# The last output tile in three pieces on two store queues, and three input loads issued as two DMAs each

## The chip, the cores and the metric

The kernel runs on one core of a Trainium2 chip. Its time is the device time of an execution in microseconds (us). TensorE (PE in the profile) does the matrix products; VectorE (DVE), ScalarE (ACT) and GpSimd (POOL) do elementwise work; SyncE (SP) computes nothing here and issues DMAs. ScalarE and GpSimd can issue DMAs too.

## The reference

Two layers in a row: a decayed linear attention, and a two-layer perceptron on its output. Inputs and output are float32.

```python
B, H, S, D = 4, 8, 768, 64                # attention, in blocks of 64 positions
for b in range(S // 64):
    intra = einsum('bhic,bhjc->bhij', qb, kb) * Dmask      # lam ** (i - j), i >= j
    intra = einsum('bhij,bhjd->bhid', intra, vb)
    inter = einsum('bhid,bhde->bhie', qb * lam_pow, kv_state)
    out[:, :, block] = intra + inter
    kv_state = lam_block * kv_state + einsum('bhsd,bhse->bhde', kb * rev_pow, vb)
x = out.transpose(0, 2, 1, 3).reshape(3072, 512)
h = x @ w_in                               # 512 -> 2048
g = h + sin(alpha * h) ** 2 / (alpha + 1e-9)
result = g @ w_out                         # 2048 -> 512, output (3072, 512)
```

## The kernel before, in words

**Tiles and stages.** The 3072 rows of the perceptron are worked in six groups g of 512. The attention comes in 24 units u, four to a group, each one half of the heads for 256 positions of one batch. For a unit, q, k and v come in as three loads of 256 KB (`ld{u}q`, `ld{u}k`, `ld{u}v`, issued by `load`, line 467, on SP's queue, each into one of three staging slots of its kind), are cast to bfloat16 (`cq`, `ck`) or scaled (`sv`), and q and k are transposed, in later units by a DMA transpose (`dt{u}`, line 519). The matmuls of a unit are `step{u}` on TensorE; `oe` writes its part of the transposed activations `xt`.

For each group, sixteen `f1_g_f` (four matmuls of 128x512 each, line 684) make one 128-row slice of the hidden layer in PSUM; `sn` takes the sine (line 694), `sq` the square (line 699), and `g` puts the sum into slice f of the tile `gall` (line 707). Then four output tiles m of 128 rows follow: `f2_g_m_j`, j = 0 to 3, adds four of the sixteen slices each (`f2mm`, line 712), `ev` copies the result from PSUM to an output tile `ob` in SBUF (line 729), and `out_g_m` stores it (`f2st`, line 748) in two DMAs of 64 rows, one for each parity of the row.

**Order.** The order on every engine is written out by hand: the table `SEQ` lists the operations of PE, DVE, ACT, POOL and SP. `Plan.run` (line 47) walks these five lists with estimated durations; it chooses buffers and PSUM banks (`take`, `give`) and the order in which the program is emitted, not the order on an engine. Four PSUM banks `f` and three `part` tokens limit the running sums, three slots the output tiles. The framework puts in the semaphores from what reads and writes what.

**The end.** The last output tile to be computed is (g, m) = (5, 3). `make_f2_end` (line 935) makes it in two halves of 256 columns: `f2_5_3_0a` to `3a` early, in the middle of other tiles, evicted by ACT as `end0`, stored by `send0`; and `f2_5_3_0b` to `3b` as the very last matmuls, evicted by DVE as `end1` into an output tile of its own, stored by `send1`, whose two DMAs go to SP's queue and ACT's. Just before them on TensorE stands the tile (5, 0): `ev_5_0` on ACT, `out_5_0` in two DMAs on SP.

The end of the program (line 1067 in the profile) waits on SP for the semaphores of all DMAs.

Of the kernel before, what the change touches and what calls it, by code (L numbers as in the profile page):

```python
# [12 lines left out]
FP32 = mybir.dt.float32  # L13
# [16 lines left out]
class Plan:  # L30
# [11 lines left out]
    def add(self, *a, **k):  # L42
        op = Op(*a, **k)
        self.ops.append(op)
        return op
# [100 lines left out]
def kernel(  # L146
# [12 lines left out]
    P = nc.NUM_PARTITIONS  # L159
# [4 lines left out]
    NG = B * S // 512  # L164
    HH = H // 2
    HP = H // 2
    DM, DFF = moe_w_in.shape
# [38 lines left out]
        "DVE":  # L206
# [17 lines left out]
        "ACT":  # L224
# [52 lines left out]
    }  # L277
    QS = set()
    CK0 = [("ACT", .62), ("DVE", .43)]
    RING = 3  # L280
    NQK = 4
    NQT = 4
# [35 lines left out]
    outp = ctx.enter_context(tc.tile_pool(name="outp", bufs=1))  # L318
# [4 lines left out]
    V, G, A, SY = nc.vector, nc.gpsimd, nc.scalar, nc.sync  # L323
# [3 lines left out]
    def where(u):  # L327
        g, r = divmod(u, 4)
        bb, hh = divmod(r, 2)
        tp, bp = divmod(g, 2)  # L330
        return g, tp, 2 * bp + bb, bb, hh

    plan = Plan({"f": ["f0", "f1", "f2", "f3"], "s": ["s"], "okv": ["okv"],
                 "st0": list(range(RING)), "st1": list(range(RING)), "st2": list(range(RING)),
                 "qk": list(range(NQK)), "qt": list(range(NQT)),
                 "vb": list(range(NVB)), "sm": list(range(NSM)), "s1": list(range(NML)),
                 "s2": list(range(NML)), "ob": list(range(NOB)), "part": list(range(NPART))})
    add = plan.add
# [9 lines left out]
    def slot(op, pool_, kind, shape, dt, name=None):  # L348
        name = name or kind
        return pool_.tile(shape, dt, name=name, tag=f"{name}{op.bank[kind][0]}")  # L350

    def sync_dep(ins, after):
        tc.add_manual_dep(ins.ins, after.ins.name, mybir.DependencyInfo(
            mybir.DependencyClass.Sync, mybir.DependencyReason.DATA))
# [28 lines left out]
    for c in range(2):  # L383
# [4 lines left out]
        out=mask[:], in0=it[:].rearrange("p two e -> p (two e)").unsqueeze(1)  # L388
# [66 lines left out]
    def load_w_in(op, a, w):  # L455
        op.ins = G.dma_start(
            out=w_in_sb[:, :, a:a + w],
            in_=moe_w_in[:, a:a + w].rearrange("(c p) g -> p c g", p=P))

    def load_w_out(op, a, n):  # L460
        op.ins = G.dma_start(
            out=w_out_sb[:, a:a + n, :],
            in_=moe_w_out[a * P:(a + n) * P, :].rearrange("(f p) d -> p f d", p=P))
# [3 lines left out]
    def load(op, u, i, gate):  # L467
        _, tp, b, _, hh = where(u)
        src = (q, k, v)[i]
        tl = slot(op, stagep, f"st{i}", [P, HH, 2, D], FP32, "st_" + "qkv"[i])  # L470
        src = src[b, hh * HH:(hh + 1) * HH, tp * W:(tp + 1) * W, :]
        op.ins = SY.dma_start(
            out=tl[:].rearrange("p h two e -> p (h two e)"),
            in_=src.rearrange("h (p two) e -> p h (two e)", two=2))
        if gate is not None:
            sync_dep(op.ins, gate.ins)
        T[u, "qkv"[i]] = tl

    def cast(op, u, j):
        if j == 0:  # L480
            T[u, "qk"] = slot(op, work, "qk", [P, 2, 2, HH, D], BF16)
        o = T[u, "qk"][:, j]
        i = T[u, "qk"[j]][:].rearrange("p h two e -> p two h e")
        if j == 0 and u in QS:
            hh = where(u)[4]
            ENGINE[op.eng].tensor_tensor(
                out=o, in0=i, in1=E[:, :, hh * HH:(hh + 1) * HH].unsqueeze(3)
                .to_broadcast([P, 2, HH, D]), op=ALU.mult)
        elif op.eng == "ACT":
            A.copy(out=o, in_=i)  # L490
        else:
            ENGINE[op.eng].tensor_copy(out=o, in_=i)  # L492
# [219 lines left out]
    def f2mm(op, first, g, m, j, cols=slice(0, DM)):  # L712
        if j == 0 and op.lent is None:
            op.tile = bank(op, "f", [P, DM], FP32, "ops")
        elif j == 0:
            kind, i, head = op.lent
            if kind == "s":
                op.tile = ps.tile([P, DM], FP32, name="ops", tag=f"s{i}")
            else:
                if i == 0:  # L720
                    head.both = new_okv(head)
                op.tile = head.both[:, i]
        n = NFC // 4
        for f in range(j * n, (j + 1) * n):
            op.ins = nc.tensor.matmul(  # L725
                out=first.tile[:, cols], lhsT=gall[g][:, f, m * P:(m + 1) * P],
                rhs=w_out_sb[:, f, cols], start=(f == 0), stop=(f == NFC - 1))
# [2 lines left out]
        op.tile = slot(op, outp, "ob", [P, DM], FP32)  # L730
        A.copy(out=op.tile[:], in_=first.tile[:])  # L731

    def f2end(op, first, cols):
        op.tile = slot(op, outp, "ob", [P, DM], FP32)
        o = op.tile[:, cols]
        if op.eng == "ACT":
            A.copy(out=o, in_=first.tile[:, cols])
        else:
            V.tensor_copy(out=o, in_=first.tile[:, cols])

    def f2send(op, ev, g, m, cols, queues):
        _, tp, b, _, _ = where(4 * g + 2 * (m // 2))
        r0 = b * S + tp * W + (m % 2) * C
        rows = out[r0:r0 + C, cols].rearrange("(p two) d -> two p d", two=2)
        for par in range(2):
            queues[par].dma_start(out=rows[par], in_=ev.tile[par * D:(par + 1) * D, cols])

    def f2st(op, ev, g, m):
        _, tp, b, _, _ = where(4 * g + 2 * (m // 2))
        r0 = b * S + tp * W + (m % 2) * C  # L750
        rows = out[r0:r0 + C, :].rearrange("(p two) d -> two p d", two=2)
        for par in range(2):
            SY.dma_start(out=rows[par], in_=ev.tile[par * D:(par + 1) * D, :])


    PEL = 0.22
    on = lambda e, c: [(e, c)]
    for i in range(NWARM):
# [8 lines left out]
        first = dop if i <= NLAM else first  # L767
# [36 lines left out]
    def make_unit(u):  # L804
        _, tp, b, bb, hh = where(u)
        lq, lk, lv = ld[u]
        early = u < NT
        cq = add(f"cq{u}", CQS if u in QS else CQ if u else CK0, [lq, tbm if u in QS else None],
                 lambda op: cast(op, u, 0), take=("qk",), give=((lq, "st0"),),
                 gives={"qk": 3 if u not in DMAT else 2})  # L810
        ck = add(f"ck{u}", CK if u else CK0, [lk, cq], lambda op: cast(op, u, 1),
                 give=((lk, "st1"),))
# [121 lines left out]

    def make_f2_end(g, m):
        prev = None
        for k, cols in enumerate((slice(0, DM // 2), slice(DM // 2, DM))):
            first = None
            for j in range(4):
                deps = [f1_done[g, f][None] for f in range(4 * j, 4 * j + 4)]  # L940
                op = add(f"f2_{g}_{m}_{j}{'ab'[k]}", on("PE", .44), deps + [prev], None,
                         take=("f", "part") if j == 0 else (), lag=PEL if j == 3 else -0.05, mode="n")
                first = first or op
                op.emit = lambda op, j=j, first=first, cols=cols: f2mm(op, first, g, m, j, cols)
                prev = op
            if k == 0:
                ev = add("end0", on("ACT", .4), [prev], lambda op, first=first, cols=cols:
                         f2end(op, first, cols), take=("ob",), give=((first, "f"), (first, "part")))
                add("send0", on("SP", 1.0), [ev], lambda op, ev=ev, cols=cols:
                    f2send(op, ev, g, m, cols, (SY, SY)))  # L950
            else:
                ev = add("end1", on("DVE", .35), [prev], lambda op, first=first, cols=cols:
                         f2end(op, first, cols), take=("ob",))
                add("send1", on("SP", 1.0), [ev], lambda op, ev=ev, cols=cols:
                    f2send(op, ev, g, m, cols, (SY, A)))

    def make_f2(g, m):
# [39 lines left out]
    for x in WX:  # L997
        j, a = done[x], at[x]
        n = (WI if x == "i" else WO)[j]
        if x == "i":  # L1000
            op = add(f"wi{j}", on("POOL", .8), [],
                     lambda op, a=a, n=n: load_w_in(op, a, n), dma=(NDC * P / 16 * dw(n), dw(n)))
            wi.update((f, op) for f in range(a // P, (a + n) // P))
        else:
            op = add(f"wo{j}", on("POOL", .2 * n), [],
                     lambda op, a=a, n=n: load_w_out(op, a, n), dma=(n * P / 16 * .081, .081))
# [65 lines left out]
```

## Time and profile before

| What | Value |
|---|---|
| Time, median of three runs | 215.83 us (215.66 to 216.15) |
| Span of the profiled execution, first to last instruction | 214.5 us |
| Median less that span | 1.3 us |
| TensorE, busy share of the span | 96% |
| ScalarE, VectorE, GpSimd | 65%, 56%, 61% |
| Granted TensorE clock | 1.000 |
| HBM read, written | 27.27 MB, 6.29 MB |

The profile comes from one execution; its own time is given as the span. What lies outside the span, before the first and after the last instruction, is in the timed runs alone. Times in a view count from the span's start. An instruction line of the timeline reads: start, length, engine, source line, operation, tiles. "SPq" and "ACTq" are DMAs being issued; the data move later.

### The profile page before, as it was taken

Reading aid. Unit: us, or ns where it says so; the run is one execution under the profiler, and the core shown is the slowest. Engines: PE = TensorE matmul, PEld = TensorE weight load, DVE = VectorE, ACT = ScalarE, POOL = GpSimd, SP = SyncE. Lnnn points to the kernel's source line nnn. Section 1 sums busy time; section 2 is a strip of 40 time slices with the busy share of each in tenths; the row PEclk is TensorE's granted clock in tenths of the full one; section 3 lists DMA queues with packets and bytes.
Section 4 is the critical chain, followed back from the end, with each engine's and each line's share of the span. In section 5 each row is a group of like instructions: output and inputs, shape, how many; then the busy total and the mean of one; then the engine's idle time right before and its main releaser. Section 6 shows DMA issues by size and latency. Waiting matters only on the chain.

```text
span 214.5 us, 5205 instructions
## 1 busy us (share of the span) xinstructions
PE 205.4 (96%) x2037; PEld 106.5 (50%) x2066; DVE 119.4 (56%) x174; ACT 138.8 (65%) x251; POOL 131.2 (61%) x212
## 2 busy tenths in 40 slices
PE   8988999999999999999999999999999999999992
PEld 3666444455445555455555555554444444444551
DVE  2387775466488774676968868766455313212100
ACT  3574788555799668878888789466578746335030
POOL 7899899288899699898979998430441030003000
PEclk9999999999999999999999999999999999999999
DMA  5999999999999999999966743040240022041553
GB/s 156 300 288 202 209 180 158 290 237 292 280 262 246 218 195 191 326 283 234 263 169 161 176 92 68 3 89 16 44 98 2 0 52 49 0 93 43 112 121 78
DMA packets 62139, 33.65 MB, mean 157 GB/s; under 512 B 17938, under 2 KB 59170, under 8 KB 62114
## 3 DMA queue, kind: packets, MB, share of 16 engines
q1 hardware_dynamic: 57776, 29.04, 57.8%
q0 software_dynamic: 4224, 4.19, 12.5%
q8 instruction: 16, 0.26, 0.5%
q10 hardware_dynamic: 114, 0.07, 0.1%
q14 instruction: 9, 0.07, 0.1%
HBM read 27.27 MB, written 6.29 MB: 156 GB/s over the span
## 4 chain that ended last, share of the span: by engine, by line
PE 91%; DVE 2%; ACT 2%; POOL 2%; issue 1%; DVEq 0%
PE hps L689 37%; PE ops L725 35%; PE sp L532 3%; PE okv L725 3%; PE okv L655 3%; PE bz L762 3%; PE okv L642 2%; PE pt L508 1%; DVE gall L708 1%; PE okv L566 1%; POOL vb L498 1%; ACT s L696 1%; ACT s L703 1%; DVE sm L540 1%; PE kp L566 0%
## 5 line engine op out<-in xcount | busy, mean ns | idle before, releaser
L708 DVE SCALAR_TENSOR_TENSOR gall<-s,r_sb,hps 128x512 bf16<-128x512 bf16 (+1 forms) x97 | 69.6, 739 | 59.7 <-ACT s L703 42.5
L689 PE MATMUL hps<-xt,w_in_sb 128*128 128x512 bf16 (+1 forms) x367 | 90.2, 377 | 1.8 <-DVE gall L708 0.5
L696 ACT ACTIVATE s<-hps,alpha_sb 128x512 bf16<-128x512 f32 (+1 forms) x97 | 65.5, 680 | 28.2 <-PE hps L689 27.2
L725 PE MATMUL ops<-w_out_sb,gall 128*128 128x512 bf16 (+1 forms) x362 | 82.1, 370 | 0.6 <-issue 0.5
L705 POOL TENSOR_TENSOR s<-s 128x512 bf16<-128x512 bf16 x31 | 32.2, 1042 | 48.0 <-ACT s L696 45.7
L725 PEld LDWEIGHTS <-gall 128*128 128x128 bf16 x400 | 38.5, 98 | 42.1 <-DVE gall L708 0.2
L689 PEld LDWEIGHTS <-w_in_sb 128*128 128x128 bf16 x388 | 36.4, 98 | 42.0 <-issue 1.7
L703 ACT ACTIVATE s<-s 128x512 bf16<-128x512 bf16 (+1 forms) x66 | 40.3, 621 | 1.2
L540 DVE TENSOR_TENSOR sm<-sp,mask 128x1024 bf16<-128x1024 f32 x24 | 29.2, 1217 | 1.2 <-PE sp L532 1.2
L498 POOL TENSOR_TENSOR vb<-st_v,R 128x512 bf16<-128x512 f32 x24 | 25.0, 1046 | 2.0 <-DMA st_v<-in_v_dram 2.0
L731 ACT COPY ob<-ops 128x512 f32<-128x512 f32 x21 | 12.2, 585 | 19.2 <-PE ops L725 16.2
L594 POOL TENSOR_TENSOR kvbd<-kvx,LBD 128x256 bf16<-128x256 f32 x32 | 19.6, 614 | 2.5
L674 DVE TENSOR_TENSOR xt<-okv,ET 128x512 bf16<-128x512 f32 x24 | 16.5, 686 | 6.3 <-ACT kva L576 4.0
L591 POOL TENSOR_TENSOR kvx<-kva,kvs 128x128 f32<-128x128 f32 x32 | 14.6, 457 | 7.1 <-ACT kva L576 7.0
L492 POOL CAST qk<-st_k 128x512 bf16<-128x512 f32 x18 | 10.9, 615 | 4.1 <-DMA st_k<-in_k_dram 4.0
L532 PE MATMUL sp<-qt 64*64 64x128 bf16 x384 | 10.2, 221 | 0.5 <-DVE sm L540 0.3
L490 ACT CAST qk<-st_q 128x512 bf16<-128x512 f32 x13 | 8.0, 622 | 3.7 <-DMA st_q<-in_q_dram 3.7
L655 PE MATMUL okv<-sm,vb 64*64 64x128 bf16 x384 | 9.7, 218 | 0.5 <-DVE sm L540 0.5
L762 PE MATMUL bz<-const-bfloat16-1.0 128*128 128x256 bf16 (+1 forms) x33 | 9.4, 401 | 0.8 <-PEq L1056 0.8
L515 ACT COPY qt<-pt 128x512 bf16<-128x512 bf16 x11 | 6.4, 591 | 5.1 <-PE pt L508 5.1
L576 ACT COPY kva<-okv 128x256 f32<-128x256 f32 (+1 forms) x16 | 5.1, 316 | 6.9 <-PE okv L566 6.9
L632 POOL TENSOR_TENSOR kvs<-kvx,ET 128x128 f32<-128x128 f32 x24 | 9.4, 405 | 0.0
(63 smaller groups left out, 110.1 us busy)
## 6 DMA issues: line engine op xcount, KB each, us to landing
st_k<-in_k_dram SPq DMA_DIRECT2D x24, 256.0 KB, 4.4
st_q<-in_q_dram SPq DMA_DIRECT2D x24, 256.0 KB, 4.5
st_v<-in_v_dram SPq DMA_DIRECT2D x24, 256.0 KB, 4.4
out_dram<-ob SPq DMA_DIRECT2D x46, 128.0 KB, 2.4
w_out_sb<-in_moe_w_out_dram POOLq DMA_DIRECT2D x4, 512.0 KB, 8.3
w_in_sb<-in_moe_w_in_dram POOLq DMA_DIRECT2D x2, 512.0 KB, 6.7
w_in_sb<-in_moe_w_in_dram POOLq DMA_DIRECT2D x1, 768.0 KB, 9.8
w_in_sb<-in_moe_w_in_dram POOLq DMA_DIRECT2D x1, 256.0 KB, 6.6
```

What stands on the lines that cost most here:

```text
L498: ENGINE[op.eng].tensor_tensor(out=T[u, "vb"][:], in0=T[u, "v"][:].rearrange("p h two e -> p two h e"), in1=R[:, :, hs].unsqueeze(3).to_br ...
L532: nc.tensor.matmul(out=T[u, "sp"][half[c], hd, par, hp, :], lhsT=QT[half[hd], 1, par, hp, half[c]], rhs=QT[half[hd], 0, :, hp, half[c]], s ...
L540: V.tensor_tensor(out=T[u, "sm"][:].rearrange("p hd par hp i -> p (hd par) hp i"), in0=T[u, "sp"][:].rearrange("p hd par hp i -> p (hd par ...
L594: G.tensor_tensor(out=bd[:], in0=X.unsqueeze(2).to_broadcast([P, 2, 2, D]), in1=LBD[:, hs, :].unsqueeze(3).to_broadcast([P, 2, 2, D]), op= ...
L655: nc.tensor.matmul(out=okv[half[hd], c, hp * P:(hp + 1) * P], lhsT=VB[half[c], par, 2 * hp + hd, :], rhs=ST[half[c], hd, par, hp, :], star ...
L674: V.tensor_tensor(out=o, in0=i, in1=ET[:, 2 * hh:2 * hh + 2].rearrange("p hp two e -> p hp (two e)") .unsqueeze(1).to_broadcast([P, 2, 2, ...
L689: op.ins = nc.tensor.matmul(out=op.tile[:, cols], lhsT=w_in_sb[:, c, f * P:(f + 1) * P], rhs=xt[g][:, c].rearrange("p b c i -> p (b c i)") ...
L696: A.activation(out=op.tile[:, cols], in_=mm.tile[:, cols], func=ACTF.Sin, scale=alpha_sb[:, f:f + 1])
L703: A.activation(out=op.tile[:, cols], in_=s1, func=ACTF.Square)
L705: ENGINE[op.eng].tensor_tensor(out=op.tile[:, cols], in0=s1, in1=s1, op=ALU.mult)
L708: V.scalar_tensor_tensor(out=gall[g][:, f, cols], in0=sq.tile[:, cols], scalar=r_sb[:, f:f + 1], in1=mm.tile[:, cols], op0=ALU.mult, op1=A ...
L725: op.ins = nc.tensor.matmul(out=first.tile[:, cols], lhsT=gall[g][:, f, m * P:(m + 1) * P], rhs=w_out_sb[:, f, cols], start=(f == 0), stop ...
```

## The change

- The last output tile is made in three pieces, of 256, 128 and 128 columns, where it was two of 256. The second and third stand at the end of TensorE's order, one after the other; each takes a PSUM bank and a `part`, and DVE evicts both (`end1`, `end2`) into the output tile that `end0` took. `send1` and `send2` store them, each in one DMA on SP's queue and one on ACT's.
- `out_5_0` puts its second DMA on ACT's queue instead of SP's.
- Three loads, v of unit 22 and k and v of unit 23, are issued as two DMAs of two heads each, one right after the other, instead of one of four heads. The tile and its readers stay the same.
- The planned durations of the new operations are set to match.

```diff
 SEQ, PE:  ... f2_5_3_0b f2_5_3_1b f2_5_3_2b f2_5_3_3b
+          f2_5_3_0c f2_5_3_1c f2_5_3_2c f2_5_3_3c
 SEQ, DVE: ... g_5_9_None end1
+          end2
 SEQ, SP:  ... out_5_2 send0 out_5_1 out_5_0 send1
+          send2
+    SPLIT = {(22, 2), (23, 1), (23, 2)}
...
     def load(op, u, i, gate):
-        op.ins = SY.dma_start(
-            out=tl[:].rearrange("p h two e -> p (h two e)"),
-            in_=src.rearrange("h (p two) e -> p h (two e)", two=2))
+        n = HH // 2 if (u, i) in SPLIT else HH
+        for h in range(0, HH, n):
+            op.ins = SY.dma_start(
+                out=tl[:, h:h + n].rearrange("p h two e -> p (h two e)"),
+                in_=src[h:h + n].rearrange("h (p two) e -> p h (two e)", two=2))
...
-    def f2end(op, first, cols):
-        op.tile = slot(op, outp, "ob", [P, DM], FP32)
+    def f2end(op, first, cols, whole=None):
+        op.tile = whole.tile if whole else slot(op, outp, "ob", [P, DM], FP32)
...
     def f2st(op, ev, g, m):
+        if (g, m) == (NG - 1, 0):
+            f2send(op, ev, g, m, slice(0, DM), (SY, A))
+            return
...
     def make_f2_end(g, m):
-        for k, cols in enumerate((slice(0, DM // 2), slice(DM // 2, DM))):
+        for k, cols in enumerate((slice(0, DM // 2), slice(DM // 2, 3 * DM // 4),
+                                  slice(3 * DM // 4, DM))):
...
-                ev = add("end1", on("DVE", .35), [prev], lambda op, first=first, cols=cols:
-                         f2end(op, first, cols), take=("ob",))
-                add("send1", on("SP", 1.0), [ev], lambda op, ev=ev, cols=cols:
+                ev = add(f"end{k}", on("DVE", .3), [prev], lambda op, first=first, cols=cols:
+                         f2end(op, first, cols, ev0), give=((first, "f"), (first, "part")))
+                add(f"send{k}", on("SP", .55), [ev], lambda op, ev=ev, cols=cols:
                     f2send(op, ev, g, m, cols, (SY, A)))
```

More of the change, by code (lines that the diff above doesn't have):

```diff
@@ L940, in make_f2_end @@
                 deps = [f1_done[g, f][None] for f in range(4 * j, 4 * j + 4)]
-                op = add(f"f2_{g}_{m}_{j}{'ab'[k]}", on("PE", .44), deps + [prev], None,
-                         take=("f", "part") if j == 0 else (), lag=PEL if j == 3 else -0.05, mode="n")
+                op = add(f"f2_{g}_{m}_{j}{'abc'[k]}", on("PE", .22 if k else .44), deps + [prev],
+                         None, take=("f", "part") if j == 0 else (), lag=PEL if j == 3 else -0.05, mode="n")
                 first = first or op
@@ L946, in make_f2_end @@
             if k == 0:
-                ev = add("end0", on("ACT", .4), [prev], lambda op, first=first, cols=cols:
+                ev = ev0 = add("end0", on("ACT", .4), [prev], lambda op, first=first, cols=cols:
                          f2end(op, first, cols), take=("ob",), give=((first, "f"), (first, "part")))
```

6 rows, old and new, of the table SEQ are left out of this document.

## The prediction

> **What bounds the kernel now.** I read the page's table of engines first, then the chain that ended last, then the end of the span in the timeline, the waits of the DMA queue and the closing instructions.
>
> ```profile
> PE 205.4 (96%) x2037; PEld 106.5 (50%) x2066; DVE 119.4 (56%) x174; ACT 138.8 (65%) x251; POOL 131.2 (61%) x212
> PE 91%; DVE 2%; ACT 2%; POOL 2%; issue 1%; DVEq 0%
> ```
>
> TensorE is busy for 96% of the span and is 91% of the chain. From 63 us to its last matmul the starts of its matmuls leave no gap longer than 0.18 us, save those of 0.22 to 0.32 us where a record is missing. So a change in the middle can't gain; it can only make TensorE wait. What is left is the tail after the last matmul:
>
> ```profile
> 207.83 2.62 PE ops L725 x20
> 210.54 0.42 DVE ob L739
> ```
> ```profile
> 208.32 2.12 PE L725 MATMUL ops<-w_out_sb,gall 128*128 128x512 bf16 x17
> 208.78 0.59 ACT L731 COPY ob<-ops 128x512 f32<-128x512 f32 x1 [2.05 <-PE ops L725]
> 209.39 1.11 SPq L753 DMA_DIRECT2D out_dram<-ob  x2
> 210.99 0.47 SPq L746 DMA_DIRECT2D out_dram<-ob  x1
> 210.99 0.55 ACTq L746 DMA_DIRECT2D out_dram<-ob  x1
> ```
> ```profile
> L1067 SPq EVENT_SEMAPHORE  x2: 28/28/28, 211.5 to 212.3; - x2
> L1067 SPq EVENT_SEMAPHORE  x7: 28/28/28, 213.2 to 213.6; - x7
> ```
>
> The first fence is the end of the chain (start, length), the second the timeline from 208.5 us, the third SP's closing waits before and after 213.1 us. Tail in numbers: matmuls end at 210.44; the eviction takes 425 ns to 210.96; both stores are issued at 210.99. By the packet records SP's store moves data from 212.11 to 212.57 and ACT's from 212.40 to 212.86; 0.36 us later, at 213.22, SP's wait for the ACT store passes. Then come more waits. SP waits at the end for eight store semaphores in a fixed order; the instruction records name them:
>
> ```
> 211.51 118,117   212.30 100,116   213.22 103,115   213.29 105,114   213.35 106,113
> 213.41 107,112   213.47 108,111   213.53 109,102   213.59 110,104   213.66 drain, 214.49 end
> ```
>
> From 212.30 to 213.22 SP waits for 103, the ACT store, third in the list; six waits that were long satisfied follow at 0.061 us each. The same records show how DMAs get semaphores: every DMA of SP and ACT takes the next of 100, 103, 105, 106, 107, 108, 109, 110, in a ring (the nine output DMAs before the last pair took 100, 103, 105, 106, 107, 108, 109, 110, 100; the last pair 103 on ACT and 105 on SP). So the number of DMAs ahead of a store decides its place in the closing list.
>
> **The change, part by part.** The sum is made on the profiled execution, span 214.49 us. The three timed runs have a median of 215.83, 1.34 more; nothing here touches what lies outside the span, so I take the saving off the median.
>
> *PE.* 16 matmuls of 256 columns become 32 of 128. The 256-column starts are 109.2 ns apart, and the first is at 208.53. For 128 columns the nearest row is eight transposes in a row:
>
> ```profile
> 43.54 0.61 PE L508 MATMUL pt<-iden,qk 128*128 128x128 bf16 x8
> 43.33 0.65 PEld L508 LDWEIGHTS <-qk 128*128 128x128 bf16 x8
> ```
>
> Less the 0.22 us of the last one, 0.39 us over seven steps is 55.7 ns, each with its own weight load. The last start moves from 208.53 + 15 x 0.109 = 210.17 to 208.53 + 31 x 0.0557 = 210.26; a 128-column matmul is recorded with 219 ns instead of 272, so the end moves from 210.44 to 210.48: +0.04. Bounds: the spacing can't be under 53 ns (the slope between 109.2 at 256 columns and 215.8 at 512, times 128), -0.05; at 98 ns, a weight load's recorded length, without overlap, it is +1.35. I take 55.7, as it is measured on this shape. The page "TensorE: Matmul & The Clock Gate" of the Trainium skill, section Back-to-back issue gap, gives about 81 ns for a sustained stream of load and matmul pairs at 128 columns; by that the end moves by +0.82 and the whole sum is +0.28. The trace's runs of eight and four do not agree, but they are shorter than 32. The third piece needs a PSUM bank and a "part": those of f2_5_2, of the first piece and of f2_5_1 are evicted by 206.7, before 208.5, so that costs nothing; with f2_5_0's (evicted 209.37) it would still be in time.
>
> *Last eviction.* 128 columns instead of 256. VectorE copies from PSUM took 425 ns (256 columns) and 173 ns (16), 1.05 ns a column: 291 ns, -0.134. The middle eviction starts at about 209.69 and ends at 209.98, before the last at 210.57, so it is hidden. Both now write into the first piece's output tile. That removes a wait (the old tile's earlier store landed at 209.8, unseen behind the matmuls). If writes waited for a store that reads other columns of the tile, this would cost; but g_5_9 is written into gall at 198.5 while TensorE reads gall without a gap (196.43 to 210.4), so other parts of one tile don't wait. Cost zero.
>
> *Issue.* out_5_0's second DMA goes from SP (209.91 to 210.50) to ACT at 209.4, where only the last stores follow it. SP is free from 209.86, so send1 goes out at 210.0 on both queues (0.47 and 0.55) and send2 at 210.89, 0.10 earlier than now (0.04 - 0.134). If that DMA stayed on SP, send1 would wait until 210.5; send2 would not.
>
> *Last data.* Each last store is 64 rows of 512 B instead of 1024.
>
> ```profile
> out_dram<-ob SPq DMA_DIRECT2D x46, 128.0 KB, 2.4
> out_dram<-ob SPq DMA_DIRECT2D x3, 64.0 KB, 2.0
> out_dram<-ob ACTq DMA_DIRECT2D x1, 64.0 KB, 2.2
> ```
>
> Issue to landing is 2.4 us at 128 KB, 2.0 to 2.2 at 64. The packet records have a median of 74 ns for 1024 B and 27 for 512 B (loads), four packets to an engine: up to 0.19 less. Bounds 0 and -0.2 (another 64 KB row step halved). I take -0.10, the middle, because the packets also come staggered over 0.4 us. Queued ahead are out_5_0 (now done at 211.94, then about 211.8) and send1's 64 KB (about 0.3 us), done by 212.1, while send2's data can't start before 210.89 + 1.12 = 212.01 on SP and 212.30 on ACT; so no more than 0.1 of queueing, within the bounds. The page "DMA: Bandwidth & Descriptors", Rules for kernel authors, of the Trainium skill says that under 64 KB one mostly pays overhead, and that spreading over queues only saves issue time; by that this term is 0 and the sum -0.40. The 0.4 us between the 128 KB and 64 KB rows speaks for some gain.
>
> *Closing waits.* Three split loads add three DMAs, the third piece two. With the ring shifted by three, out_5_2 takes 107 and 108, send0 109 and 110, out_5_1 100 and 103, out_5_0 105 and 106, send1 107 and 108, send2 109 and 110: the last to land stand last in the list, and the satisfied waits pass while SP waits anyway. If ACT has 109 (it had the lower number before), one wait is left instead of six: 5 x 0.061 = -0.305; with 110, -0.367. Bounds: -0.37, and +0.06 at the second place. I take -0.305.
>
> *Split loads.* ld22v goes out at 105.03; its second half ends SP's issuing at about 106.1, hidden by SP's wait for ACT until 107.8; its reader runs at 130.6. ld23k goes out at 116.24 and lands in 3.1; GpSimd reads it at 121.05, 1.65 us after its landing at 119.4, and a second issue costs 0.4 to 0.6. ld23v is read at 131.6. Behind them on SP stands dt20 at 117.96, then up to 1 us later; it lands in 4.0, so by about 123, and step20 runs at 126.05; dt21 waits for GpSimd until 121.13 anyway. A DMA waits for the one eight earlier in the ring, now up to three closer: those were issued 5 us or more before, and land in 4.4. The two or three added semaphore waits on GpSimd (about 0.05 each) run ahead of its work. All of it zero; without the cover, up to 1 us.
>
> Sum: 0.04 - 0.134 - 0.10 - 0.305 = -0.50. 215.83 - 0.50 = 215.33.
>
> **Rivals.**
> - *Weight loads bound the narrow matmuls* (slower). Place: the 32 matmuls from 208.53. For: each load is recorded with 98 ns, more than the 55.7 it must hide in, and no run of the trace is longer than eight. Against: the eight. At 98 ns the end is 1.35 later: 1.35 - 0.54 = +0.81, 216.64; it loses from 72 ns a matmul on (31 x 16 ns = 0.50). By the 81 ns of the Trainium skill's page named above (TensorE: Matmul & The Clock Gate, Back-to-back issue gap) it would be 216.11.
> - *The rotation doesn't come out* and send2's semaphores stand early in the list: only the eviction and the data count, -0.20, 215.63. For: the last pair took its two numbers in reverse, so the assignment isn't plain order. Against: all others from 3 us on are strict.
> - *The pieces wait for each other's stores* through the shared tile: end2 waits for send1's landing (210.0 + 2.2 = 212.2) instead of 210.57, +1.6 - 0.5 = +1.1, 216.9. Against: gall, above.
> - *A late load holds TensorE up*: from 1.65 us on at ld23k, or 3 us at dt20; a miss of 1 us gives 216.3. Against: the slack above, at every reader.
>
> **How the numbers follow.** About 0.2% (0.43 us) is what a measurement of this kernel can tell from no change. Forecast 0.70: its own range, with the bounds of the data (0 to -0.2) and of the closing waits and a run-to-run spread of 0.2, is 214.9 to 215.7; -0.50 lies little beyond 0.43, so 0.56 of it is faster, 0.14 within. Rotation 0.12: 0.10 within, 0.02 faster. Weight loads 0.11: 0.02 within (spacing up to 85 ns), 0.09 slower. Shared tile 0.04, slower. Late load 0.03, slower. Faster 0.58, same 0.26, slower 0.16. The range goes from 214.9 to 216.15, which takes in a spacing up to 82 ns (0.82 more) and leaves the dearer cases out.
>
> **What would show it.** Right: 128-column matmuls about 56 ns apart, ending near 210.5; a last eviction near 0.29; stores at about 210.9; after the last landing (near 213.0) one or two closing waits instead of seven; TensorE without gaps from 110 to 150. Wrong: a spacing over 72 ns, an eviction that waits for a DMA, closing waits in a row after the last landing, or a later step20 to step23.

## The result, and the profile after

The changed kernel took 215.27 us (median of 13 runs, 215.04 to 215.97), the kernel before beside it 216.14 (13 runs, 215.66 to 217.10). The ratio is 0.9967, 95% interval 0.9953 to 0.9981: 0.33% faster, 0.7 us, with 0.4 to 1.0 in the interval. The forecast was 0.50 us less, which lies in the interval, and 215.33. That 215.27 comes so near to 215.33 is luck: the forecast was taken off the first three runs' 215.83, and the kernel before took 0.31 more in the runs beside. The profiled execution has a span of 214.02 us, 0.47 less than before.

The page: TensorE's share of the span and of the chain is what it was, and only the number of its instructions grew.

```profile
PE 205.2 (96%) x2053; PEld 106.5 (50%) x2082; DVE 119.7 (56%) x175; ACT 138.9 (65%) x251; POOL 131.4 (61%) x212
PE 91%; DVE 2%; ACT 2%; POOL 2%; issue 1%
```

The timeline of the end:

```profile
208.43 2.17 PE L728 MATMUL ops<-w_out_sb,gall 128*128 128x512 bf16 x33
...
208.89 0.59 ACT L734 COPY ob<-ops 128x512 f32<-128x512 f32 x1 [2.05 <-PE ops L728]
209.50 1.92 SPq L749 DMA_DIRECT2D out_dram<-ob  x3
209.51 2.06 ACTq L749 DMA_DIRECT2D out_dram<-ob  x3
209.74 0.29 DVE L742 COPY ob<-ops 128x128 f32<-128x128 f32 x1 [10.36 <-PE ops L728]
210.63 0.29 DVE L742 COPY ob<-ops 128x128 f32<-128x128 f32 x1 [0.60 <-PE ops L728]
```

Two short evictions stand where one of 0.42 stood, and three stores go out close together on each of the two queues: an issue chain of 1.9 and 2.1 us. ACT's has no pause longer than 0.10 us; SP's has one of 0.33 before the last store. SP's closing waits, up to 213.04 us and after it:

```profile
L1074 SPq EVENT_SEMAPHORE  x7: 28/28/28, 211.5 to 212.7; - x7
L1074 SPq EVENT_SEMAPHORE  x2: 28/28/28, 213.1 to 213.1; - x2
```

Seven waits pass while the last store is under way, two after it; before, it was two and seven.

Executions differ ahead of this tail: the first of the last matmuls (the b and c pieces) starts anywhere from 207.8 to 209.1 us in the twelve profiled executions of this study, though all that precedes it on TensorE is the same, and the first hidden-layer matmul already from 19.0 to 20.1. That is more than the whole effect. So I read the tail from the start of the first of these matmuls ("zero" below), by the instruction records, and use the times only to see that they agree.

| From zero, us | before | after | difference | forecast |
|---|---|---|---|---|
| end of the last matmul | 1.910 | 1.950 | +0.04 | +0.04 |
| end of the last eviction | 2.428 | 2.279 | -0.149 | -0.094 |
| ACT's last store issued | 2.460 | 2.360 | -0.100 | -0.094 |
| that store landed (its wait passes) | 4.690 | 4.412 | -0.278 | -0.194 |
| end of the span | 5.958 | 5.375 | -0.583 | -0.499 |

From the landing to the end it is 1.268 before and 0.963 after: -0.305, the five waits at 0.061.

### The profile page after: what moved, and what is told of

It reads as the page before. It is cut to its first block, busy times and chain, and to the rows that moved or that the text cites. A ratio compares the mean times of both kernels' runs of the same rounds, so it can differ in the third digit from the quotient of the medians.

```text
span 214.0 us, 5247 instructions
## 1 busy us (share of the span) xinstructions
PE 205.2 (96%) x2053; PEld 106.5 (50%) x2082; DVE 119.7 (56%) x175; ACT 138.9 (65%) x251; POOL 131.4 (61%) x212
## 4 chain that ended last, share of the span: by engine, by line
PE 91%; DVE 2%; ACT 2%; POOL 2%; issue 1%
PE hps L692 38%; PE ops L728 36%; PE sp L535 3%; PE okv L728 3%; PE okv L658 3%; PE bz L768 3%; PE okv L645 2%; PE pt L511 1%; DVE gall L711 1%; PE okv L569 1%; POOL vb L501 1%; ACT s L699 1%; ACT s L706 1%; DVE sm L543 1%; PE kp L569 0%
## 5 line engine op out<-in xcount | busy, mean ns | idle before, releaser
L728 PE MATMUL ops<-w_out_sb,gall 128*128 128x512 bf16 (+2 forms) x378 | 82.1, 361 | 0.6 <-issue 0.5
```

The lines of the kernel that those rows point to most:

```text
L728: op.ins = nc.tensor.matmul(out=first.tile[:, cols], lhsT=gall[g][:, f, m * P:(m + 1) * P], rhs=w_out_sb[:, f, cols], start=(f == 0), stop ...
```

## The experiments

The theory was: three things add up, the shorter eviction, the lighter store, and the place of the last store in the closing waits. Rival A leaves out the place; rival B says that the split loads help the middle of the kernel. In the tables of this part "tail" is zero to the end of the span.

**1. The changed kernel with whole loads**

```diff
-    SPLIT = {(22, 2), (23, 1), (23, 2)}
+    SPLIT = set()
```

> The changed kernel with its three loads whole again, so three DMAs fewer ahead of the last stores. Theory (the ring of store semaphores decides how many closing waits follow the last landing): send2 now has 106 on ACT and 107 on SP; four satisfied waits (107 to 110) follow the landing of 106 where the changed kernel has one, so 3 x 0.061 = 0.18 us more than the changed kernel between last landing and end; all else alike; time 0.3 us under the kernel before instead of 0.5. Rival A (the gain is the shorter last eviction and store alone): no difference to the changed kernel. Rival B (the split loads help the middle of the kernel): the middle is slower, the last matmul starts later, by a few tenths.

Measured: 0.9979 of the kernel before (0.9965 to 0.9993). Tail 5.577, 0.202 more than the changed kernel; the last store landed at 4.434, 0.02 later, and five waits follow from it on instead of two. These are SP's closing waits from 212.6 us:

```profile
L1074 SPq EVENT_SEMAPHORE  x5: 27/28/28, 212.7 to 212.9; - x5
```

0.180 of the 0.202 lies between landing and end, as forecast (0.18). The last matmul starts 1.730 after zero in this and in the changed kernel, and zero itself is not later (208.24 against 208.65), so nothing speaks for rival B; with zero scattering over 1.3 us this alone can't exclude a few tenths.

**2. The kernel before with five split loads**

```diff
 (load as in the changed kernel)
+    SPLIT = {(22, 0), (22, 1), (22, 2), (23, 1), (23, 2)}
```

> The kernel before, untouched at its end, with five loads (q, k, v of unit 22, k and v of unit 23) issued as two DMAs each. Theory: the last pair of stores moves from 103 and 105 to 109 and 110, one wait follows the landing of 109 instead of six: 5 x 0.061 = 0.305 us less between last landing and end, 0.14% of the time; eviction, issue and landing as before. Rival A: no gain at all. Rival B: gain in the middle, so an earlier last matmul.

Measured: 0.9982 (0.9965 to 1.0000). Tail 5.674, 0.284 less than before: the eviction still takes 0.425 us and the store lands 2.22 after its issue (2.23 before), but only two waits are left, here from 213.3 us on:

```profile
L1070 SPq EVENT_SEMAPHORE  x2: 28/28/28, 213.4 to 213.4; - x2
```

Rival A falls: a kernel whose end is not touched gains 0.28 us by DMAs that are issued 100 us earlier.

**3. The kernel before with eight split loads: one whole turn of the ring**

```diff
+    SPLIT = {(20, 0), (20, 1), (22, 0), (22, 1), (22, 2), (23, 0), (23, 1), (23, 2)}
```

> The kernel before with eight loads split (also q and k of unit 20 and q of unit 23): eight more DMAs are one whole turn of the ring. Theory: the last pair has 103 and 105 again, seven closing waits from the last landing on, no gain over the kernel before. Rival A: no gain either. Rival B: more gain than with five.

Measured: 1.0003 (0.9986 to 1.0021). Tail 5.941; seven waits from the landing on, as before:

```profile
L1070 SPq EVENT_SEMAPHORE  x7: 28/28/28, 212.8 to 213.2; - x7
```

Rival B falls too: more split loads, no gain; the interval reaches no further than 0.3 us.

**4. The changed kernel with five split loads**

```diff
-    SPLIT = {(22, 2), (23, 1), (23, 2)}
+    SPLIT = {(22, 0), (22, 1), (22, 2), (23, 1), (23, 2)}
```

> The changed kernel with five split loads instead of three, so its last pair gets 100 on ACT and 103 on SP, at the second and third place of the closing waits. Theory: seven satisfied waits follow the landing of 100 instead of one, 6 x 0.061 = 0.37 us more than the changed kernel; only 0.27 of the saving of its pieces is left against the kernel before (0.1 to 0.2%). Rivals A and B: the same as the changed kernel or faster.

Measured: 0.9993 (0.9977 to 1.0010), so no gain over the kernel before that can be told. Tail 5.720, 0.345 more than the changed kernel (0.37 expected). From 212.9 us on:

```profile
L1074 SPq EVENT_SEMAPHORE  x8: 27/28/28, 213.0 to 213.4; - x8
```

Two DMAs too many in the ring take back more than half of the change's saving.

**5. out_5_0's second DMA back on SP's queue**

```diff
-            f2send(op, ev, g, m, slice(0, DM), (SY, A))
+            f2send(op, ev, g, m, slice(0, DM), (SY, SY))
```

> The changed kernel with out_5_0's second DMA back on SP's queue. The ring is the same (send2 on 109 and 110). The prediction's step said that send1 would then wait on SP until about 210.5 and send2 not at all. In the changed kernel send1's issue takes SP 0.55 us and ACT 0.8, so SP would be busy until 211.1: send2's SP store goes out 0.15 to 0.2 us late. Theory: the ACT store still lands last (SP's landed about 0.25 earlier), so the cost is 0 to 0.1 us; ACT's send1 has nothing ahead of it and may be issued sooner. Rival (the second queue for out_5_0 is where the gain lies): 0.3 us or more is lost.

Measured: 0.9998 (0.9975 to 1.0021). Tail 5.701, 0.326 more than the changed kernel: the theory's 0 to 0.1 was wrong, and the rival's 0.3 was met. The timeline of the end:

```profile
209.89 2.56 SPq L749 DMA_DIRECT2D out_dram<-ob  x4
...
210.45 1.37 ACTq L749 DMA_DIRECT2D out_dram<-ob  x2
211.03 0.29 DVE L742 COPY ob<-ops 128x128 f32<-128x128 f32 x1 [0.60 <-PE ops L728]
```

SP issues four stores in a row, with pauses of 0.1 us or less. Its part of send1 goes out at 211.10, where ACT's part went out at 210.45, and takes 0.72 us, with an issue on ACT beside it from 0.25 us on; its part of send2, just as close behind but with ACT idle, takes 0.54. So send2 goes out on SP 2.879 after zero, not 2.306, and is now the last to land. Of these 0.57 us, send1's later start makes 0.64 and its longer issue 0.17, less 0.24 of a pause that is used up.

**6. The second queue without the third piece**

```diff
 (the kernel of experiment 2)
     def f2st(op, ev, g, m):
+        if (g, m) == (NG - 1, 0):
+            f2send(op, ev, g, m, slice(0, DM), (SY, A))
+            return
```

> The kernel before with five split loads (so the last pair has 109 and 110) and out_5_0's second DMA on ACT's queue; the last tile stays in two halves. Against the same kernel without the ACT queue (5.674 us from the first of the last matmuls to the end) it shows what that queue alone is worth, and against the changed kernel (5.375) what the third piece is worth once the queue is free. Theory (the queue only makes room for send1): no difference to 5.67, within 0.05; so the third piece is worth 0.3 with the queue, and nothing without it. Rival (the second queue is a gain by itself, as out_5_0 lands sooner): 5.4 to 5.5.

Measured: 0.9997 (0.9980 to 1.0015). Tail 5.709, 0.035 more than with the queue left alone: no gain from the queue by itself. Against the kernel before the tail is 0.25 us shorter, which would make 0.9988 and lies in the interval. The timeline of the end:

```profile
209.53 2.12 SPq L749 DMA_DIRECT2D out_dram<-ob  x2
209.53 2.15 ACTq L749 DMA_DIRECT2D out_dram<-ob  x2
210.73 0.42 DVE L742 COPY ob<-ops 128x256 f32<-128x256 f32 x1 [11.32 <-PE ops L728]
```

Each stretch of two issues has one of about 0.5 us at either end; both queues are free from 210.1 on, long before the eviction ends at 211.16, so making room brings nothing here. All four kernels here have their last pair on 109 and 110:

| tail, us | out_5_0 on SP alone | on SP and ACT |
|---|---|---|
| two pieces | 5.674 | 5.709 |
| three pieces | 5.701 | 5.375 |

Neither part is worth anything without the other. Together they are worth 0.30. Each number is from one trace. How far a tail repeats is seen twice: the changed kernel has 5.375 in both of its traces (experiment 10), and the kernel before and experiment 3, whose last stores take the same places, have 5.958 and 5.941.

**7. Pieces of 256, 192 and 64 columns**

```diff
-        ... slice(DM // 2, 3 * DM // 4), slice(3 * DM // 4, DM)
+        ... slice(DM // 2, 7 * DM // 8), slice(7 * DM // 8, DM)
```

> The changed kernel with pieces of 256, 192 and 64 columns, to see what a load and matmul pair costs at 64 columns, half the width at which 31 steps of 55.7 ns were seen. If the columns alone bind, the 16 last matmuls stand 29 ns apart and TensorE ends as before; if a weight load of 128 columns binds, they stand at 50 to 56 ns and TensorE ends 0.3 to 0.4 us later. The last eviction is 224 ns instead of 292. send1 goes out about 0.4 us later, and its issue (0.55 on SP, 0.8 on ACT) then stands in front of send2: the end is 0.2 to 0.4 us later than the changed kernel's.

Measured: 0.9991 (0.9973 to 1.0008). Tail 5.495, 0.12 more than the changed kernel, less than expected. TensorE ends 1.950 after zero as there: the columns bind, not the loads, down to this width. The groups between 209.9 and 211.5 us (busy time and mean ns after the bar; the mean is one instruction's recorded length, not the distance of two starts):

```profile
L728 PEld LDWEIGHTS <-gall 128*128 128x128 bf16 x22 | 1.1, 98 | 0.0
...
L728 PE MATMUL ops<-w_out_sb,gall 128*128 128x64 bf16 x16 | 0.6, 193 | 0.0
```

Sixteen matmuls of 64 columns, each with a load of its own that is recorded with 98 ns, take 0.6 us in all: by the records they start 29 ns apart.

**8. Four pieces**

```diff
-        ... slice(3 * DM // 4, DM)
+        ... slice(3 * DM // 4, 7 * DM // 8), slice(7 * DM // 8, DM)
-    SPLIT = {(22, 2), (23, 1), (23, 2)}
+    SPLIT = {(23, 2)}
 (and a fourth end and send in the lists)
```

> Four pieces of 256, 128, 64 and 64 columns with one split load instead of three, so that the last pair again has 109 and 110. Theory (the queues' issue time is the next limit): the last eviction is 0.07 shorter, but three stores of 0.5 to 0.8 us of issue each follow within 0.9 us of matmuls, so the last pair goes out at about 211.6 instead of 210.95 and the end is 0.4 to 0.7 us later than the changed kernel's. Rival A (a shorter last eviction and store is the gain): another 0.1 us gained.

Measured: 0.9989 (0.9972 to 1.0006). Tail 5.752, 0.377 more than the changed kernel, just under the 0.4 to 0.7 expected. The timeline:

```profile
209.47 2.39 SPq L749 DMA_DIRECT2D out_dram<-ob  x4
209.47 2.70 ACTq L749 DMA_DIRECT2D out_dram<-ob  x4
...
210.64 0.23 DVE L742 COPY ob<-ops 128x64 f32<-128x64 f32 x1 [0.24 <-PE ops L728]
```

The last eviction ends at 210.87, but the queues are busy: SP gets to the last store at 211.31 and ACT at 211.62. The finer cut loses to the issue of its own stores, as the theory said; rival A falls once more.

**9. One DMA for each piece of the last tile**

Experiments 5 and 8 point to the number of DMAs. Two are needed for each piece because its two row parities lie in the two halves of the partitions. Here the rows are put in order where `gall` is written, and one DMA of 128 rows stores a piece.

```diff
 f1g, for g = 5, as two instructions: columns 0 to 384 as they were, and
+            o = gall[g][:, f, 384:512].rearrange("p (q two) -> p two q", two=2)
+            (in0 and in1 of these columns: "p (two q) -> p two q")
 f2send, for (g, m) = (5, 3):
+            SY.dma_start(out=out[r0:r0 + C, cols], in_=ev.tile[:, cols])
+            return
-    SPLIT = {(22, 2), (23, 1), (23, 2)}
+    SPLIT = {(22, 0), (22, 1), (22, 2), (23, 0), (23, 1), (23, 2)}
```

> A candidate beyond the changed kernel. The rows of the last tile are put in natural order where gall is written (its last 128 columns by a second VectorE instruction for each slice of group 5), so that each of its three pieces is stored by one DMA of 128 rows on SP's queue instead of two of 64; out_5_0 stays on two queues. Six loads are split so that send2 has 110, the last place of the closing waits. If the ACT store's late data (0.27 us after SP's of the same issue) are what sets the last landing, then one DMA on SP lands 0.1 to 0.2 us sooner, and no satisfied wait follows, another 0.06: the end comes 0.15 to 0.25 us sooner after the first of the last matmuls than in the changed kernel (5.375 there). If the 128 descriptors of one DMA take as long as two times 64, only the 0.06 is left. The 16 added VectorE instructions lie in its idle time.

Measured: 214.90 us, 0.9946 (0.9927 to 0.9965), the fastest kernel here. Tail 4.926, 0.449 less than the changed kernel, twice what was expected. The timeline, and SP's closing waits from 212.15 us on:

```profile
209.00 0.47 SPq L757 DMA_DIRECT2D out_dram<-ob  x1
209.01 0.55 ACTq L757 DMA_DIRECT2D out_dram<-ob  x1
209.24 0.29 DVE L747 COPY ob<-ops 128x128 f32<-128x128 f32 x1 [10.22 <-DMA out_dram<-ob]
209.57 1.22 SPq L753 DMA_DIRECT2D out_dram<-ob  x2
210.14 0.29 DVE L747 COPY ob<-ops 128x128 f32<-128x128 f32 x1 [0.60 <-PE ops L733]
```
```profile
L1082 SPq EVENT_SEMAPHORE  x1: 27/27/27, 212.2 to 212.2; - x1
```

The last store goes out 2.306 after zero, as SP's did in the changed kernel, takes 0.34 us to issue, and lands 1.74 later, where the pair on two queues took 2.11 from SP's issue: -0.37. Of this, 0.26 is what ACT's part landed after SP's in the changed kernel; SP's part by itself had taken 1.83 there. From the landing to the end it is 0.88 instead of 0.96, with one wait less: the other -0.08. The rule "Two transfers to disjoint partition halves" of the Trainium skill (DMA: Bandwidth & Descriptors, Rules for kernel authors) says to use one transfer of 128 partitions, as the halves share the same engines. This experiment agrees, with 0.37 us for 64 KB; it also uses one queue where there were two and has half as many DMAs of the tile ahead of the last, and no run separates these.

**10. The changed kernel again, beside 6 and 9**

> The changed kernel as it is, beside the two above on the same chip: 0.3% under the kernel before, 5.37 us from the first of its last matmuls to the end, one wait after the landing of 109.

Measured: 215.54 us, 0.9983 (0.9963 to 1.0004); the tail is 5.375 again. The interval is wider and touches 1; it holds 0.9973, what 0.583 us make.

## Why the prediction was right, and where it was off

- **TensorE: right.** 31 steps of 55.7 ns and +0.04 at the end, as forecast from eight transposes. The rival that weight loads bind, and the 81 ns of the Trainium skill's page (TensorE: Matmul & The Clock Gate, Back-to-back issue gap), are not borne out here: 55.7 ns over 31 steps at 128 columns, and 29 ns at 64.
- **Last eviction: right in size** (292 ns against 291). It also starts sooner after TensorE's end, 0.037 us instead of 0.093. In the kernel before, the records show a separate wait instruction ahead of the copy, for TensorE and for an older store; in the changed kernel the copy itself waits for TensorE. The forecast had put the removed wait at nothing. The 0.05 did not reach the end: ACT's issue of send1 ended at 210.911, 0.014 before the eviction, and its next issue started 0.095 later, 0.054 after SP's.
- **Issue: the number was right by luck, the reason half wrong.** The forecast had the last store out 2.36 us after zero, right behind the last eviction, and ACT's went out at 2.360. But the eviction ended 0.055 sooner than forecast, and what held ACT was its issue of send1, 0.82 us where 0.55 was put down; the two misses cancel. The step also said that with out_5_0's second DMA on SP send1 would wait and "send2 would not". Experiment 5 shows send2 late on SP by 0.57, and 0.33 us lost. The step stopped at the wait of the first store and did not carry it through that store's issue to the next. In the sum the queue stood as mere cover; in the table of experiment 6 the pieces' whole gain depends on it.
- **Last data: mis-sized.** -0.10 was taken between 0 and -0.20; from ACT's issue to the landing it went from 2.230 to 2.052, -0.178. By the packet records the last store's data took 0.30 us instead of 0.45, started 0.07 sooner after the issue, and the wait passed 0.05 later after the last packet. The difference holds over the runs: 2.22 to 2.25 wherever the two last stores have 64 KB each, 2.05 to 2.09 where they have 32 KB and go out within 0.06 us of each other. The Trainium skill's rule that the prediction weighed here (DMA: Bandwidth & Descriptors, Rules for kernel authors: mostly overhead under 64 KB) was read there as a term of 0; this difference does not agree with that reading. The next halving does not go on in the same way: with 16 KB ACT's store took 2.05 in experiment 7 and 1.80 in experiment 8, where SP's went out 0.04 and 0.31 us ahead of it. So the bytes alone do not set this time, and what else does stays open. This term is nearly the whole gap between the forecast 0.50 and the measured 0.58.
- **Closing waits: right**, -0.305 in both, with ACT on 109 and SP on 110. Experiments 1 to 4 put the last pair at four places of the list and found 2, 5, 7 and 8 waits from the landing on.
- **Split loads: right in their cost, none.** dt20 was issued at 119.19 instead of 117.96, 1.2 us later (0.1 of it the shift of the whole execution), a little more than the 1 us allowed; TensorE was busy for 39.53 us of the stretch from 110 to 150 before and after.
- **Rotation and shared tile: neither rival came.** In the changed kernel end2 follows its matmuls by 0.04 us, while send1, the store of the tile's other columns, is under way (issued at 210.07, landed at 212.59). end1 follows by 0.04 too, but send0 had landed by then.

What stays open is where the 1 us from execution to execution ahead of the tail comes from; no run here was made for that. Two things were never varied alone: the shorter eviction and the lighter store, which always came together with the third piece.

## What to carry to other kernels

At the end of a program read what comes after the last landing too: completed semaphores are still waited for one by one, and in this program, where the DMAs of SP and ACT take eight semaphores in turn, which DMA stands last in that list can be turned by DMAs anywhere before it. Count the issue time of stores that follow one another closely, on each queue and with both at work, before cutting a last tile finer: pieces and queue were worth 0.30 us together and nothing apart. Fewer DMAs beat more of them: one of 128 rows for each piece, with send2 in the last place of the list, gave another 0.45.

## What the runs showed of the hardware that was not expected

- How long an issue takes depends on what was issued just before. In the kernel before, with ACT idle, a store of 64 rows on SP took 0.47 to 0.49 us after a pause of 0.4 us or more, and 0.49 to 0.62 within 0.1 us of the issue before it, save two that took 1.4 and 1.8. So SP's 0.55 for send1 in the changed kernel is no more than SP takes by itself. Two cases go beyond it: ACT's 0.78 to 0.82 for an issue close behind another while SP issues close behind another too (send1 in the changed kernel; the last store in experiment 7), where ACT's send2 in the changed kernel, beside an issue of SP's that came after a pause, took 0.56; and SP's 0.72 in experiment 5 beside ACT. That the two queues hold each other up there is likely; no run had ACT issue two stores in a row with SP idle.
- ACT's data start later than SP's where the two issues are about 0.05 us apart or less: 212.34 against 212.07 in the changed kernel, 212.40 against 212.11 before.
- A stream of matmuls, each with a new 128x128 bfloat16 weight, ran at 29 ns a pair with 64 columns (experiments 7 and 8), though each load is recorded with 98 ns.
